# One product per pair of heads for the carried state, shift of 20 weight pieces on ScalarE, in a state-space scan followed by two feed-forward blocks

## The chip, the cores and the metric

The program runs on one core of a Trainium2 chip. The metric is device time in microseconds (us) for one execution; each kernel is executed several times and the median counts. One execution is recorded by the hardware profiler; its rows are the trace. Engines: PE is TensorE's matmul queue and PEld its weight loads, DVE is VectorE, ACT is ScalarE, POOL is GpSimd, SP issues most of the transfers.

## The reference

Three computations follow one another. The first is a state-space scan over 4 batches, 8 heads, 768 positions, head width D = 32 and state width N = 16. In chunks of positions:

```python
M = (Cc @ Bc.T) * L                 # L: causal decays inside the chunk
y = M @ xc + (Cc @ state) * decay_to_i
state = decay_full * state + (Bc * decay_from_j).T @ xc
```

Its output (3072 tokens, 256 features, a head being 32 of them) goes through `g = elu(x @ w_in)`, `x2 = g @ w_out` (256 to 2048 to 256), and then through `((x2 @ w1) * (x2 @ w2)) @ w3 @ wo2` (width 1024).

## The kernel before, in words

**Precision.** Large products are made from a high and a low word of each operand (type fp32r): `mm3` issues three matmuls, low weights by high data, high by low, high by high (lines 382, 383, 384). The small products of the scan are plain fp32 matmuls, and the trace shows each of them as two records.

**Stages.** Six tiles of 512 tokens (NTILE) are each four chunks of 128 positions (CPT); a chunk has two halves `s` of R = 64 positions. For a pair of chunks `unit_u` makes C·B (line 521) and the state increments u (line 556), and `unit_y` makes y: 32 matmuls within the halves (line 590), then 32 that add what the carried state gives (line 598). `made_x` evacuates y from PSUM as high words (ScalarE in the first two tiles, VectorE after) and low words (VectorE); it is letter z, its second step Y. For each tile and each of 8 column blocks n of `w_in`, `unit_a` (letter a) makes h, `elu` its activation in five steps on ScalarE and VectorE, and `unit_b` (b) multiplies by `w_out`. `half_a` (v) is the early form of a: it makes h of the first 256 tokens of tile 0 alone, so that TensorE need not wait for chunks 2 and 3; a later `unit_a` then makes the other half only. The first four column blocks of tile 0 use plain fp32 words in `unit_b` (line 745).

The second half of the program (letters c e g G E ( ) and d) forms the last block by products of sums of blocks: seven `by_product` products per column m of w1 and w2, and `last_product` (d). Results of c, G, E and ) share PSUM room m % 2, so the c of column m+2 waits until `gate_1` (line 902, letter >) of column m has read that room; VectorE runs it in a queue with the sums (lines 893, 896) and the low words (line 162).

**State.** A tile `st` holds the states of 8 heads: 128 partitions are four head pairs of 2 × 16 rows, and the 2 × 32 columns are both heads' features. The product Bx of a pair also fills the blocks that mix the two heads, and these are not wanted. Before, `cd` (C by the decays, made on GpSimd by `at_cd`) is stored with zeros for the other head, 2 × 64 columns per half, and the line 598 product is issued once per head g, with the 32 columns of `st` that belong to it.

**Weights.** They arrive as 44 pieces of 128 × 512 words of 64 bits packed in halves; `shifted` (letter k, VectorE, line 210) and `scaled` (j, ScalarE, line 214) prepare both halves of each word, `joined` (K, VectorE) merges them, `his` (H, ScalarE) takes high words and `los` (I) low words.

**Order.** The string ORDER is written out, one letter per step; `in_order` keeps each engine's instructions in that order. What stands before an instruction on its engine, and what it waits for, thus follows from the string.

Of the kernel before, what the change touches and what calls it, by code (L numbers as in the profile page):

```python
# [37 lines left out]
094AAlU7AlC5Al5UCJCD566l8jCNk5K8JkHND6IjDQjND6KkHNkKQzzYNYzIvzjYNYjkaKjk!HaKXjkxIkNjKarkKMjsHMxKbIrNKxsXrLaHkBjLN8j8vsxX  # L38
BHKuWkPIrbDHMKjkIMKbWINsRXaWHLCNjLBbxCDrCttBjNsCakhVkiyxIrKbXkzsWzMHYYuhKNIaHiXIDbxDNrttjsyVaKzXzkHYYhNVaIxijMrkKbMsHxPL
raINhLjsaxijNhRbxXrLCCiaMSBSBrsBCbshxirLahKBiaxksHrIkbjsxCNKrKuHksbhItDVahtDjijykxirbMKHsMzbzhYPiNYuhKbXHtDtDjkyLaBzIzYY  # L40
INiaxKrXLHbHIsxNkhIRa1jBrMiaCxNCsrKwXxshkNribfsjCXjKHuFhMIatjDHNLIakxCDSiSr1bKxtLNrwsjskykfHFKhIaMzzHKjINibBkMBxYKYbhNri
PsuhbXjDtiXwtkDLykfhFRaHXHIziBNbxIYjLrwzBsNYKukHMfIbjFDMKtHNaDILXCkwxBLCNhtrKajsfjKhiaxiHrkIbFKHxINsrbhskyhSwPjzzYYMKiaH
XSIijMfBakxCFNHCrIaXxsrRwxsrsbfjKkFLahBiuLxbrtBDCHDItbshiKyhHbzXIzYi1CuhYMaDDXttwixMrLBafNLsbBxCFrCkNjsyhazijYkbKxzKr3Y%
&su&h=bitbhtD&D=y=S&Saz=YNziaxYrsaNh3xibxkrrbsshiahjijKbxkK%&ra&s^=hb=&ix&=ar=Nsax1rh3aNxirksb3jxKs@jakK%&=a@#&h3rib&s@&
=x=b=h#Nri^ahs^xia@N#rk#jxsbrKsaSkjSKh%b@i&=xb^h&@=#ahi&ribx#s3r1xsb&=h3^@iar=hbix/srsbh/i|ch_bmi/|#b_/G|e]_gncS[Em({|G}
)]_e>gn<c[*Em(.{G})],<e.>En,g.{*c[,(m)S}*g.1>e.,*G[<3nc,.d*](,mE.}G.{d.,<e],)ng>E,.c{[*dm,(G*.}d.<e]*,d$.d,$),ng>.d+*.(,
[dc,$E}.d@{em,<@d#nG#d*3]g@+)[#^(>E}*c@{e.<dn^dm+d@#G.,)]#*g$>E@(.#^[c{3.d}*m),.e.,G<ng>](,@^E[}c,dm,e.#g.,Gd,*]d{E+n*).
<d.{d[*,(>d)+*c}d+m<e.,2gn>3G[+(]c.}dm,E.3,d.,G.,d,*g{e<dn*)+.(]+2*d.}E.>[d{.c,<2em,).Gn*>g],d.,d.,c[E,md,*({G}*.d<]).e*
>$d,.g*n,c[d.+($,2dm,E.}G.,d]{e$,<)@+gn#d[*(>@E}.*c{e<dn#d.,^)m+d@.g#^@G>.d,@*d+@d#](^.,E[c{*dm}).#G<.>e@#dng]#c[,Em,({G
}g],).,e,*En>d[d+*.d{c<*dm,).+(.*G>.g}.d],<[e+En+2c.,dm{(d}d,G,e]<)$,g.+*dn>2[d,c*.+(.d}*.d,2mE,G*.e{d,n<).,d.>g](,[c,E}  # L50
m*d{e*dnG.)],(.>*d$}E.<g.,d.{[c,<$d+me$,2).g,d+[d>nG.d.d.+c],(mE}d,e{G,nd+]),g<(>.d$[d.Ed{}),<d>,d..,d,dd+++++
"""
HALF = 4
VECTOR_LO = 16
PIECES = [(("w_in", "w_out")[k == "o"], "iioiooiiiiooiooo"[:n].count(k)) for n, k in enumerate("iioiooiiiiooiooo")] + [("wo2", m) for m in range(4)] + [("w3", m) for m in range(16)] + [
# [36 lines left out]
XCOLS = (("x", DM), ("bn", NH * N), ("bt", 2 * R), ("cz", 2 * 2 * R), ("cp", SUB * 2 * R))  # L92
# [3 lines left out]
def kernel(  # L96
# [42 lines left out]
    side = const.tile([P, 2], F32, name="side")  # L139
    sel = act.tile([P, 2, 2, TT], F32R, tag="g", name="sel")[:SUB * CPT, 0, 0].rearrange("p (k s i) -> p k s i", k=CPT, s=SUB)  # L140
    begun = const.tile([P, CPT * SUB, R], F32, tag="begun", name="begun")

    def constants():
# [11 lines left out]
        G.memset(begun, 0.0)  # L155

# [35 lines left out]
    class Piece:  # L192


        def __init__(self, name, src, room, dst):
            self.name, self.src, self.room, self.dst = name, src, room, dst
            self.lo, self.word, self.parts, self.half = G, None, None, 0

# [232 lines left out]
    def at_load(k):  # L431
        c = ck[k]
        all_ = att.tile([P, XC], F32, tag="xbc", name=f"xbc{k}", bufs=4)
# [9 lines left out]
        c["cp"] = cols_["cp"].rearrange("p (s f) -> p s f", s=SUB)  # L443
# [99 lines left out]

    def turned(k, p):

        return (p + k % 2) % 4

    def u_products(k, u):
# [3 lines left out]
        for p in range(4):  # L552
            for s in halves(k):
                rows = slice(R * s, R * s + R)
                to = turned(k, p)
                T.matmul(u[32 * to:32 * to + 32, s], c["bd"][rows, 2 * p:2 * p + 2].rearrange("p h n -> p (h n)"),
                         c["x"][rows, 64 * p:64 * p + 64], start=True, stop=True, skip_group_check=True)

    def states(k, u):
# [4 lines left out]
        for s in halves(k):  # L564
            V.scalar_tensor_tensor(out=new[:, s], in0=state[k, s], scalar=pr_of(k)[:, s, R - 1:R], in1=u[:, s],
                                   op0=ALU.mult, op1=ALU.add)
            state[(k, 1) if s == 0 else (k + CPT, 0)] = new[:, s]

    def first_states(k, u):
# [3 lines left out]
        state[k, 1], state[k + CPT, 0] = new[:, 0], new[:, 1]  # L573
        later("8", next_state, k)

    def next_state(k):

        kept = att.tile([P, 2 * D], F32, tag="kept", name=f"kept{k}", bufs=1)
        G.tensor_tensor(out=kept, in0=state[k, 1], in1=ck[k]["pr"][:, 1, R - 1:R].to_broadcast([P, 2 * D]), op=ALU.mult)
        G.tensor_tensor(out=state[k + CPT, 0], in0=state[k + CPT, 0], in1=kept, op=ALU.add)  # L580

    def y_products(*chunks):
        for k, both in chunks:
            c = ck[k]
            for g in range(2):
                for s in range(SUB):
                    rows = slice(R * s, R * s + R)
                    for q in range(4):
                        h = 2 * q + g
                        T.matmul(both[32 * q:32 * q + 32, s, g], c["x"][rows, D * h:D * h + D], c["L"][rows, h],  # L590
                                 start=g == 0, stop=(k, s) not in state, skip_group_check=True)
# [15 lines left out]
    def by_head(y):  # L607
        return y.rearrange("p s (g i) -> p s g i", g=2)
# [500 lines left out]
```

## Time and profile before

| | us |
|---|---|
| median of 3 runs | 525.79 (524.62 to 525.8) |
| profiled execution | 524.71 |
| span of its trace | 523.0 |
| TensorE busy | 508.8 |
| VectorE busy | 428.8 |
| ScalarE busy | 323.6 |
| GpSimd busy | 204.4 |

The span is what the trace covers; 1.7 us of the profiled execution lie around it. The granted clock of TensorE is 1.0 over the whole span.

### The profile page before, as it was taken

To read this page: it belongs to the slowest core of one execution; us is meant where nothing else is said; L and a number is where in the kernel's file an instruction comes from. 1 tells how busy PE (TensorE), PEld (TensorE's weight loads), DVE (VectorE), ACT (ScalarE), POOL (GpSimd) and SP (SyncE) were. 2 spreads that over 40 slices of the span, in tenths; PEclk is the share of its full clock that TensorE was granted. 3 is DMA by queue.
4 is the path that set the end of the run, shared out by engine and by line. 5 is a ranking of instruction groups with operands and counts; after the bars stand their busy time and mean duration, and the time that the engine had idled before them with its cause. 6 is when DMAs were issued, how large, how long until landed. Compare 5 with 4: busy or idle time off the path is not lost.

```text
span 523.0 us, 10654 instructions
## 1 busy us (share of the span) xinstructions
PE 508.8 (97%) x4330; PEld 411.2 (79%) x4330; DVE 428.8 (82%) x589; ACT 323.6 (62%) x482; POOL 204.4 (39%) x184
## 2 busy tenths in 40 slices
PE   5799999999999999999999999999989999999996
PEld 3675788778888888878788888888777888888885
DVE  6888989879897996867766797869999989988845
ACT  2585587655754385535476787747766577765650
POOL 3223004205430544122203333967477465755401
PEclk9999999999999999999999999999999999999999
DMA  8993473147555635053202321001000110001002
GB/s 297 348 277 132 134 207 126 41 143 235 170 158 150 222 108 174 1 160 104 69 35 77 106 80 47 35 0 61 0 22 21 61 41 20 1 20 41 21 1 80
DMA packets 28177, 52.66 MB, mean 101 GB/s; under 512 B 2304, under 2 KB 10880, under 8 KB 28128
## 3 DMA queue, kind: packets, MB, share of 16 engines
q1 hardware_dynamic: 27984, 51.85, 30.4%
q8 instruction: 34, 0.56, 0.4%
q14 instruction: 15, 0.12, 0.1%
q10 hardware_dynamic: 144, 0.13, 0.1%
HBM read 45.58 MB, written 6.39 MB: 99 GB/s over the span
## 4 chain that ended last, share of the span: by engine, by line
PE 91%; DVE 6%; issue 1%; DMA 0%; ACT 0%; DVEq 0%
PE acc L382 9%; PE acc L384 9%; PE h L382 9%; PE acc L383 9%; PE h L383 9%; PE h L384 9%; PE p L382 4%; PE p L384 3%; PE p L383 3%; PE acc L745 3%; PE p_d L382 2%; PE p_d L384 2%; PE p_d L383 2%; PE p_E L382 2%; PE p_E L383 2%; PE p_E L384 2%
## 5 line engine op out<-in xcount | busy, mean ns | idle before, releaser
L715 ACT ACTIVATE e<-h 128x1024 f32<-128x1024 f32 x48 | 49.2, 1025 | 58.0 <-PE h L384 55.5
L382 PE MATMUL h<-xTh,w_in 128*128 128x512 f32 (+1 forms) x200 | 80.0, 400 | 0.8 <-ACT xTh L685 0.8
L383 PE MATMUL h<-xTl,w_in 128*128 128x512 f32 (+1 forms) x200 | 77.7, 389 | 0.0
L384 PE MATMUL h<-xTh,w_in 128*128 128x512 f32 (+1 forms) x200 | 77.5, 388 | 0.0
L162 DVE TENSOR_TENSOR g<-e,g 128x1024 fp32r<-128x1024 f32 x44 | 60.1, 1370 | 15.5 <-ACT g L727 15.4
L382 PE MATMUL acc<-g,w_out 128*128 128x512 f32 x176 | 69.6, 396 | 0.0
L722 DVE SCALAR_TENSOR_TENSOR e<-e,h 128x1024 f32<-128x1024 f32 x44 | 53.3, 1214 | 19.7 <-ACT e L717 19.6
L384 PE MATMUL acc<-g,w_out 128*128 128x512 f32 x176 | 68.6, 390 | 0.0
L383 PE MATMUL acc<-g,w_out 128*128 128x512 f32 x176 | 68.5, 389 | 0.0
L727 ACT CAST g<-e 128x1024 fp32r<-128x1024 f32 x44 | 46.2, 1049 | 30.0 <-PE acc L384 26.5
L717 ACT ACTIVATE e<-e 128x1024 f32<-128x1024 f32 x48 | 50.7, 1059 | 0.8
L382 PEld LDWEIGHTS h<-xTh,w_in 128*128 128x128 f32 x200 | 38.6, 193 | 9.4 <-issue 1.8
L383 PEld LDWEIGHTS h<-xTl,w_in 128*128 128x128 f32 x200 | 38.5, 193 | 7.8 <-issue 0.7
L384 PEld LDWEIGHTS h<-xTh,w_in 128*128 128x128 f32 x200 | 38.6, 193 | 7.6
L162 POOL TENSOR_TENSOR w<-raw_wc,w 128x512 fp32r<-128x512 f32 x16 | 23.9, 1502 | 51.5 <-ACT w L236 48.6
L536 POOL TENSOR_TENSOR xbc<-xbc,pr 128x256 f32<-128x256 f32 (+1 forms) x24 | 22.9, 965 | 50.9 <-DMA L<-a_cut 30.7
L382 PEld LDWEIGHTS acc<-g,w_out 128*128 128x128 f32 x176 | 33.0, 188 | 7.4
L384 PEld LDWEIGHTS acc<-g,w_out 128*128 128x128 f32 x176 | 33.0, 188 | 7.0
L383 PEld LDWEIGHTS acc<-g,w_out 128*128 128x128 f32 x176 | 33.1, 188 | 6.6
L504 POOL TENSOR_TENSOR xbc<-xbc,L 128x128 f32<-128x128 f32 x24 | 15.1, 634 | 58.1 <-DVE L L498 37.7
L899 POOL TENSOR_TENSOR room_l<-room_l,room_o 128x512 f32<-128x512 f32 x12 | 19.8, 1647 | 32.8 <-DVE room_o L896 19.1
L498 DVE TENSOR_TENSOR_SCAN L<-L,eye 128x512 f32<-128x512 f32 x20 | 27.3, 1368 | 2.0 <-DMA L<-a_cut 2.0
(427 smaller groups left out, 1278.2 us busy)
## 6 DMA issues: line engine op xcount, KB each, us to landing
xbc<-in_xc SPq DMA_DIRECT2D x24, 512.0 KB, 6.3
raw_wc<-in_w3t SPq DMA_DIRECT2D x16, 512.0 KB, 4.3
L<-a_cut SPq DMA_DIRECT2D x40, 128.0 KB, 4.8
raw_wi<-in_w_in SPq DMA_DIRECT2D x8, 512.0 KB, 8.6
raw_wo<-in_w_out SPq DMA_DIRECT2D x8, 512.0 KB, 6.4
x_dram<-x SPq DMA_DIRECT2D x6, 512.0 KB, 4.9
room_s<-x_dram SPq DMA_DIRECT2D x12, 256.0 KB, 4.3
out_t<-out SPq DMA_DIRECT2D x11, 256.0 KB, 2.0
```

The source lines that it names most:

```text
L162: eng.tensor_tensor(out=lo, in0=raw, in1=hi.bitcast(F32), op=ALU.subtract)
L382: T.matmul(out, wlo, xhi, start=first, stop=False, **kw)
L383: T.matmul(out, whi, xlo, start=False, stop=False, **kw)
L384: T.matmul(out, whi, xhi, start=False, stop=last, **kw)
L498: V.tensor_tensor_scan(out=flat, data0=wide, data1=eye.rearrange("p h s -> p (h s)"), initial=0.0, op0=ALU.mult, op1=ALU.add)
L536: G.tensor_tensor(out=c["cd"][:, n:], in0=c["cd"][:, n:], in1=c["pr"].rearrange("p s (o i) -> p s o i", o=1)[:, n:].to_broadcast([P, SUB - ...
L715: A.activation(e, h, AF.Exp)
L717: A.activation(e, e, AF.Relu, scale=-1.0, bias=1.0)
L722: V.scalar_tensor_tensor(out=gt[t, n] if plain else e, in0=e, scalar=-1.0, in1=h, op0=ALU.mult, op1=ALU.max)
L727: A.copy(hi, e)
L745: T.matmul(acc, word_of(n)[:, j, es], g[:, j], start=m == 0, stop=False)
L899: GATE[m % 2].tensor_tensor(out=s["two"], in0=s["two"], in1=s["u2"], op=ALU.mult)
```

## The change

1. The carried-state product (line 598) takes both heads of a pair at once: 64 columns of `st` against one `cd` of 64 columns, without the zeros. So `st` must itself be zero outside each head's block: `own_heads` multiplies it on GpSimd by a mask `own` after each update (letter ?, 24 times). `cd` shrinks from 2 × 64 to 64 columns per half, and each chunk's load from 1024 to 896 columns. The rotation of row groups by `turned` goes away.
2. y is now laid out by feature half f over two chunks rather than by chunk over both halves; `made_x` keeps its size. Rows of `w_in` return to their natural order.
3. For 20 of the 44 weight pieces the shift of the low words runs on ScalarE (`scalar_low`) instead of VectorE.
4. ORDER is another string throughout. The order of weight pieces changes, and so does the place of the steps around the first products.

```diff
-094AAlU7AlC5Al5UCJCD566l8jCNk5K8JkHND6IjDQjND6KkHNkKQzzYNYzIvzjYNYjkaKjk!HaKXjkxIkNjKarkKMjsHMxKbIrNKxsXrLaHkBjLN8j8vsxX
...
+094AAlA75UlAl5UCJl566?jD?k5NDCkJCD6K6?!jN?DHQCK8zIkNHzYjY8NIj8QkvzNzYjYKajNkHKjvkMxKaIrMkKjaKkNsHjLMxbIrMLxNKjakrsXHKIbx
...
+SCALAR_LOW = "11000001001111000110000010001001111100011101"
...
-XCOLS = (("x", DM), ("bn", NH * N), ("bt", 2 * R), ("cz", 2 * 2 * R), ("cp", SUB * 2 * R))
+XCOLS = (("x", DM), ("bn", NH * N), ("bt", 2 * R), ("cz", 2 * 2 * R), ("cp", SUB * R))
...
+        V.tensor_reduce(out=own, in_=head.rearrange("p (b g) -> p g b", g=2), op=ALU.add, axis=AX.X)
...
         def shifted(self):
-            V.tensor_scalar(self.low, self.low, 29, None, op0=ALU.logical_shift_right)
+            if self.scalar_low:
+                A.activation(self.low, self.low, AF.Copy, scale=15 / 16 * 2.0 ** -29 * (1 - 2.0 ** -8))
+            else:
+                V.tensor_scalar(self.low, self.low, 29, None, op0=ALU.logical_shift_right)
             self.one_of_two()
...
+    def own_heads(new):
+        n = new.shape[1]
+        G.tensor_tensor(out=new.rearrange("p s (g d) -> p s g d", g=2), in0=new.rearrange("p s (g d) -> p s g d", g=2),
+                        in1=own.rearrange("p (o g e) -> p o g e", o=1, e=1).to_broadcast([P, n, 2, D]), op=ALU.mult)
...
-        for g in range(2):
-            for s in range(SUB):
-                for k, both in chunks:
-                    for q in range(4) if (k, s) in state else ():
-                        at = turned(k, q)
-                        rows = slice(32 * at, 32 * at + 32)
-                        T.matmul(both[32 * q:32 * q + 32, s, g], state[k, s][rows, D * g:D * g + D], ck[k]["cd"][rows, s, g],
-                                 start=False, stop=True, skip_group_check=True)
+        for s in range(SUB):
+            for n, k in enumerate(chunks):
+                for q in range(4) if (k, s) in state else ():
+                    rows = slice(32 * q, 32 * q + 32)
+                    T.matmul(rooms[q // 2][64 * (q % 2):64 * (q % 2) + 64, s, n], state[k, s][rows], ck[k]["cd"][rows, s],
+                             start=False, stop=True, skip_group_check=True)
```

Three places show what the new string moves. The first is ScalarE near the start: `st` are the first states, `raw_wi` a piece of w_in, `xTh0` the high words of tile 0's y. Before:

```order
L572 COPY st1_211<-f2_138 128x128
L214 ACTIVATE raw_wi0_121<-raw_wi0_121 128x512
L236 CAST w_in0_78<-raw_wi0_121 128x512
L572 COPY st2_248<-acc_f_96 128x128
L214 ACTIVATE raw_wi1_123<-raw_wi1_123 128x512
L214 ACTIVATE raw_wo0_125<-raw_wo0_125 128x512
L572 COPY st3_305<-acc_f_96 128x128
L236 CAST w_in1_79<-raw_wi1_123 128x512
L685 CAST xTh0_364<-f2_138 128x2x2x64
L685 CAST xTh0_364<-acc_f_96 128x2x2x64
```

The same place after the change:

```order
L584 COPY st1_215<-f2_144 128x128
L227 ACTIVATE raw_wi0_127<-raw_wi0_127 128x512
L221 ACTIVATE raw_wi0_127<-raw_wi0_127 128x512
L221 ACTIVATE raw_wi1_129<-raw_wi1_129 128x512
L584 COPY st2_246<-acc_f_98 128x128
L584 COPY st3_249<-acc_f_98 128x128
L227 ACTIVATE raw_wi1_129<-raw_wi1_129 128x512
L249 CAST w_in0_80<-raw_wi0_127 128x512
L696 CAST xTh0_304<-f2_144 128x2x2x64
L249 CAST w_in1_81<-raw_wi1_129 128x512
L696 CAST xTh0_304<-acc_f_98 128x2x2x64
```

Two shifts (line 221) stand on ScalarE, and the letters z of chunks 0 and 1 now stand in ORDER ahead of the second Q (the y of chunks 2 and 3), where before both Q came first.

The second place is TensorE's products h of column block 1 of tile 0. Before, h0_1 is made once by `unit_a` at 512 columns (h0_1_412, 12 matmuls, which `elu` reads), and later the second v makes a second tile of that name; this is where that one begins:

```order
L382 MATMUL h0_3_490<-xTh0_364,w_in3_81 128x512
L383 MATMUL h0_3_490<-xTl0_365,w_in3_81 128x512
L384 MATMUL h0_3_490<-xTh0_364,w_in3_81 128x512
L382 MATMUL h0_1_517<-xTh0_364,w_in1_79 128x256
L383 MATMUL h0_1_517<-xTl0_365,w_in1_79 128x256
L384 MATMUL h0_1_517<-xTh0_364,w_in1_79 128x256
```

After the change the second v stands ahead of that a, and h0_1 follows h0_0 directly, in two halves of 256 columns that are both read:

```order
L395 MATMUL h0_0_367<-xTh0_304,w_in0_80 128x256
L396 MATMUL h0_0_367<-xTl0_305,w_in0_80 128x256
L397 MATMUL h0_0_367<-xTh0_304,w_in0_80 128x256
L395 MATMUL h0_1_409<-xTh0_304,w_in1_81 128x256
L396 MATMUL h0_1_409<-xTl0_305,w_in1_81 128x256
L397 MATMUL h0_1_409<-xTh0_304,w_in1_81 128x256
```

So 12 matmuls of 256 columns (h0_1_517), which no instruction reads, leave the program.

The third place is VectorE in the second half of the program, between `gate_1` of columns 3 and 4 (line 902 before, 914 after). Before:

```order
L902 TENSOR_TENSOR room_l2_3806<-room_l2_3806,p_1_3820 128x512
L162 TENSOR_TENSOR room_h2_4032<-room_i7_3886,room_h2_4032 128x512
L893 TENSOR_TENSOR room_l0_3843<-room_i7_3886,p_0_3819 128x512
L162 TENSOR_TENSOR room_t0_4053<-room_l2_3806,room_t0_4053 128x512
L896 TENSOR_TENSOR room_o7_3880<-room_o7_3880,p_E_3822 128x512
L899 TENSOR_TENSOR room_l0_3843<-room_l0_3843,room_o7_3880 128x512
L162 TENSOR_TENSOR room_t1_4073<-room_i7_3886,room_t1_4073 128x512
L162 TENSOR_TENSOR rooms_g_4079<-room_l2_3806,rooms_g_4079 128x512
L162 TENSOR_TENSOR room_t2_4096<-room_h0_3783,room_t2_4096 128x512
L902 TENSOR_TENSOR room_l0_3843<-room_l0_3843,p_0_3819 128x512
```

After:

```order
L171 TENSOR_TENSOR room_t0_3911<-room_l2_3660,room_t0_3911 128x512
L905 TENSOR_TENSOR room_l0_3697<-room_i7_3744,p_0_3673 128x512
L171 TENSOR_TENSOR room_t1_3922<-room_i7_3744,room_t1_3922 128x512
L908 TENSOR_TENSOR room_o7_3729<-room_o7_3729,p_E_3676 128x512
L911 TENSOR_TENSOR room_l0_3697<-room_l0_3697,room_o7_3729 128x512
L171 TENSOR_TENSOR rooms_g_3928<-room_l2_3660,rooms_g_3928 128x512
L171 TENSOR_TENSOR room_t2_3949<-room_h0_3637,room_t2_3949 128x512
L946 TENSOR_TENSOR out_00_3935<-out_00_3935,acc0_480 128x512
L908 TENSOR_TENSOR room_o7_3729<-room_o7_3729,p_E_3676 128x512
L905 TENSOR_TENSOR room_l1_3749<-room_i7_3744,p_1_3674 128x512
L171 TENSOR_TENSOR rooms_g_3928<-room_l2_3660,rooms_g_3928 128x512
L914 TENSOR_TENSOR room_l0_3697<-room_l0_3697,p_0_3673 128x512
```

Between the two gates stand 8 VectorE instructions before and 11 after (the gate of column 3, room_l2, is the row just ahead of the second list). In the same stretch, from the c of column 5 to the c of column 6, TensorE has 13 products before and 15 after; from there to the c of column 7 it has 11 in both, and VectorE's instructions up to and with the gate of column 5 go from 11 to 8.

## Rows read from the trace of the kernel before

**Rows 1.** Page, busy us of each engine (share of the span), xinstructions.

```profile
PE 508.8 (97%) x4330; PEld 411.2 (79%) x4330; DVE 428.8 (82%) x589; ACT 323.6 (62%) x482; POOL 204.4 (39%) x184
```

**Rows 2.** Waits of TensorE (total, times, longest); its busy us in a window.

```profile
PE p L382 <- DVE room_l L902: 1.8, 2, 1.4
...
0.00:20.71 20.71, 12.49 (x328) 1.00 0.92 330
```

**Rows 3.** Timeline, TensorE at a y and a u block: start us, us, instruction.

```profile
56.95 0.85 PE L598 MATMUL y<-xbc,st 32*32 32x64 f32 x64
57.73 0.50 PE L382 MATMUL acc<-g,w_out 128*128 128x512 f32 x1
...
60.70 0.69 PE L521 MATMUL s<-xbc 32*64 32x128 f32 x32
61.32 0.45 PE L556 MATMUL s<-xbc 64*32 64x64 f32 x32
```

**Rows 4.** Timeline, TensorE at the start.

```profile
19.20 0.33 PE L598 MATMUL f<-xbc,st 32*32 32x64 f32 x4
...
19.31 0.33 PE L598 MATMUL f<-xbc,st 32*32 32x64 f32 x4
...
20.71 0.55 PE L382 MATMUL h<-xTh,w_in 128*128 128x256 f32 x1 [0.83 <-ACT xTh L685]
...
21.73 0.41 PE L382 MATMUL h<-xTh,w_in 128*128 128x256 f32 x1
21.94 0.41 PE L383 MATMUL h<-xTl,w_in 128*128 128x256 f32 x1
```

**Rows 5.** Timeline, TensorE from 34 to 44 us.

```profile
34.40 0.79 PE L382 MATMUL h<-xTh,w_in 128*128 128x512 f32 x1
35.03 0.40 PE L383 MATMUL h<-xTl,w_in 128*128 128x512 f32 x1
35.26 0.39 PE L384 MATMUL h<-xTh,w_in 128*128 128x512 f32 x1
...
37.53 0.28 PE L382 MATMUL h<-xTh,w_in 128*128 128x256 f32 x1
...
39.05 0.80 PE L521 MATMUL s<-xbc 32*64 32x128 f32 x32
...
40.16 3.70 PE L745 MATMUL acc<-g,words_l 128*128 128x512 f32 x8
43.70 3.60 PE L745 MATMUL acc<-g,words_h 128*128 128x512 f32 x8
```

**Rows 6.** Timeline, ScalarE at the start.

```profile
12.46 0.68 ACT L214 ACTIVATE raw_wi<-raw_wi 128x512 f32<-128x512 f32 x1
...
19.92 0.37 ACT L685 CAST xTh<-f 128x256 fp32r<-128x256 f32 x1 [0.82 <-PE acc_f L598]
```

**Rows 7.** Timeline, VectorE at the start.

```profile
12.12 1.21 DVE L498 TENSOR_TENSOR_SCAN L<-acc_f,eye 128x512 f32<-128x512 f32 x1
...
15.04 1.87 DVE L528 TENSOR_TENSOR L<-f,L 128x512 f32<-128x512 f32 x3
```

**Rows 8.** Timeline, GpSimd at the start.

```profile
9.33 0.45 POOL L536 TENSOR_TENSOR xbc<-xbc,pr 128x128 f32<-128x128 f32 x1 [7.54 <-DVE pr L464]
...
15.48 1.31 POOL L162 TENSOR_TENSOR w_in<-raw_wi,w_in 128x512 fp32r<-128x512 f32 x1 [0.18 <-ACT w_in L236]
```

**Rows 9.** Timeline, VectorE at the gates of columns 3, 4 and 5.

```profile
366.48 0.67 DVE L902 TENSOR_TENSOR room_l<-room_l,p 128x512 f32<-128x512 f32 x1
...
374.29 0.67 DVE L902 TENSOR_TENSOR room_l<-room_l,p 128x512 f32<-128x512 f32 x1
...
384.52 0.67 DVE L902 TENSOR_TENSOR room_l<-room_l,p 128x512 f32<-128x512 f32 x1
```

**Rows 10.** Groups by line and shape: busy us, mean ns | idle before, releasers.

```profile
L504 POOL TENSOR_TENSOR xbc<-xbc,L 128x128 f32<-128x128 f32 x24 | 15.1, 634 | 58.1 <-DVE L L498 37.7 <-DMA raw_wo<-in_w_out 17.5 <-issue 2.9
L565 DVE SCALAR_TENSOR_TENSOR st<-st,pr,s 128x64 f32<-128x64 f32 x36 | 9.6, 276 | 2.6 <-PE s L556 2.0
```

More of the change, by code (lines that the diff above doesn't have):

```diff
@@ L139 @@
     side = const.tile([P, 2], F32, name="side")
+    head, own = const.tile([P, NH], F32, name="head"), const.tile([P, 2], F32, name="own")
     sel = act.tile([P, 2, 2, TT], F32R, tag="g", name="sel")[:SUB * CPT, 0, 0].rearrange("p (k s i) -> p k s i", k=CPT, s=SUB)
@@ L567, in states @@
             state[(k, 1) if s == 0 else (k + CPT, 0)] = new[:, s]
+        later("?", own_heads, new[:, :len(halves(k))])
+    def own_heads(new):
+        n = new.shape[1]
+        G.tensor_tensor(out=new.rearrange("p s (g d) -> p s g d", g=2), in0=new.rearrange("p s (g d) -> p s g d", g=2),
+                        in1=own.rearrange("p (o g e) -> p o g e", o=1, e=1).to_broadcast([P, n, 2, D]), op=ALU.mult)
     def first_states(k, u):
@@ L573, in first_states @@
         state[k, 1], state[k + CPT, 0] = new[:, 0], new[:, 1]
+        later("?", own_heads, new)
         later("8", next_state, k)
@@ L578, in next_state, with y_products @@
         kept = att.tile([P, 2 * D], F32, tag="kept", name=f"kept{k}", bufs=1)
-        G.tensor_tensor(out=kept, in0=state[k, 1], in1=ck[k]["pr"][:, 1, R - 1:R].to_broadcast([P, 2 * D]), op=ALU.mult)
+        G.tensor_tensor(out=kept, in0=state[k, 1], in1=pr_of(k)[:, 1, R - 1:R].to_broadcast([P, 2 * D]), op=ALU.mult)
         G.tensor_tensor(out=state[k + CPT, 0], in0=state[k + CPT, 0], in1=kept, op=ALU.add)
-    def y_products(*chunks):
-        for k, both in chunks:
+    def y_products(chunks, rooms):
+        for n, k in enumerate(chunks):
             c = ck[k]
-            for g in range(2):
+            for f, room in enumerate(rooms):
                 for s in range(SUB):
@@ L632, in first_u @@
         for k in ks:
-            u_products(k, ck[k]["room"][0])
+            u_products(k, ck[k]["room"])
         for k in ks:
-            later("6", first_states, k, ck[k]["room"][0])
+            later("6", first_states, k, ck[k]["room"])
     def first_y(*ks):
-        y_products(*((k, ck[k]["room"][1]) for k in ks))
+        at = 2 * R * (1 + ks[0] // 2)
+        rooms = [by_chunk(room[:, :, at:at + 2 * R]) for room in first_rooms[2:]]
+        y_products(ks, rooms)
+        for f in range(2):
+            later("z", made_x, ks[0], f, rooms[f], A)
         for k in ks:
-            later("z", made_x, k, ck[k]["room"][1], A)
             later("M", at_l, CPT + k)
@@ L670, in unit_y @@
     def unit_y(k):
-        two = [(j, by_head(banks(f"y{j}")[:, :, :2 * R])) for j in (k, k + 1)]
-        y_products(*two)
-        for j, both in two:
-            later("z", made_x, j, both, A if j < 2 * CPT else V)
+        rooms = [by_chunk(banks(f"y{k}_{f}")[:, :, :2 * R]) for f in range(2)]
+        y_products((k, k + 1), rooms)
+        for f in range(2):
+            later("z", made_x, k, f, rooms[f], A if k < SCALAR_Z * CPT else V)
         if k % CPT == 0 and k // CPT + 1 < NTILE:
@@ L681, in unit_y, with made_x @@
                 later("X", at_load, j)
-    def made_x(k, both, hi_eng):
-        hi, lo = x_room(k)
+    def made_x(k, f, both, hi_eng):
+        hi, lo = x_room(k, f)
         (A.copy if hi_eng is A else V.tensor_copy)(hi, both)
@@ L1010 @@
         p.lo = V if 0 < n < VECTOR_LO else G
+        p.scalar_low = SCALAR_LOW[n] == "1"
     for k in range(CPT):
@@ L1062 @@
         cz[:, :, :, :, j, :, :, j] = c4[:, :, :, :, j]
-    c2 = C.reshape(NB, 4, 2, CPB, SUB, R, N).transpose(3, 0, 1, 2, 6, 4, 5).copy()
-    c2[:, 1::2] = np.roll(c2[:, 1::2], 1, axis=2)
-    cp = np.zeros(c2.shape[:6] + (2, R), C.dtype)
-    for j in range(2):
-        cp[:, :, :, j, :, :, j] = c2[:, :, :, j]
+    cp = C.reshape(NB, NH, CPB, SUB, R, N).transpose(2, 0, 1, 5, 3, 4)
     def by_chunk(v):
```

91 lines of the change are left out of this document (44 added, 47 removed).

## The prediction

> **What bounds the kernel now.** I read the page first. TensorE is busy 508.8 of 523.0 us, the next engine 428.8 [rows 1]. The chain of waits, the same view read from the end backwards, is almost all TensorE, so I then looked for the 14 us in which TensorE is not busy. The waits of TensorE and its timeline put 8.2 us of it ahead of the first h product at 20.71 (busy 12.49 of 20.71, [rows 2]), which waited for ScalarE's xTh [rows 4], 1.8 us at two places in the second half where VectorE's gate came late [rows 2], and most of the rest behind the last product. Between 21 and 366 us TensorE never waits. So a change can gain in three ways: fewer TensorE instructions, an earlier first h product, a shorter wait at those gates. What it moves between VectorE, ScalarE and GpSimd is worth something only there, and costs something only where it makes TensorE wait anew.
>
> **The carried-state products.** A pair of chunks runs 32 of them, 64 records, in 0.78 us (56.95 to 57.73), 12.2 ns a record [rows 3]. After the change there are 16, 32 records, with 64 columns of weights rather than 32. What does one take? The trace has no such shape with 64 columns of data. Below, 12.2 ns, the pace of the old ones. Above, 19.4 ns, which is line 521 with the same 32*64 weights but twice the data columns (0.62 us for 32 records, [rows 3]). Beyond that I need how many run at once. A record of 512 columns in plain fp32 takes 0.44 us ((43.70 - 40.16)/8, [rows 5]), so one of 64 columns takes 55 ns alone. At 12.2 ns about four and a half run side by side. The old products alternate over two chunks with row groups rotated by `turned`, and so meet 8 distinct places of 32 rows by 32 columns. The new ones meet only four (row group q, column half q % 2). If four do run side by side the price is 55/4 = 13.7 ns. If it is the number of places that sets the parallelism, half as many places give 24.4 ns and nothing is gained. At the start, where 256 columns take 0.21 us and the clock is thus 1.2 GHz (the granted clock reads 1.0 there), the same old products come 8 per 0.11 us, 13.7 ns [rows 4]. There a record alone lasts 110 ns, so eight ran at once, without any spare time per place. At 2.4 GHz the 12.2 ns is therefore the pace at which they are issued, not a limit of the places, and four places should be kept nearly full. I take 13.7 ns: 32 x 13.7 = 0.44 us, a saving of 0.34 us a pair. Ten pairs make **-3.4 us** (between -3.9 at 12.2 ns and 0 at 24.4; -1.6 at 19.4). The two pairs of the first tile have only the second half of each chunk and stand in the start, costed below.
>
> Here a rule speaks against the change. In the old code four row groups write the same PSUM bank at once, and the rate above shows that they overlap. The new code puts row groups 0 and 1 of one half into one bank, 2 and 3 into another. The Trainium skill, "TensorEngine Tiling (Array Packing)", Gotcha 1: PSUM Pressure, says that different row tiles cannot access the same PSUM bank simultaneously; by it only two of the four would run at a time, the 24.4 ns end. By that rule the old products too should have been confined to two at a time (two chunks, one bank each), and the trace does not agree with it.
>
> **Products that no one reads.** The second v of the old order comes after the a that it should have shortened, so 12 matmuls of 256 columns are made for nothing, from 37.53 to 39.05 [rows 5], less a tenth that the passage to the small products takes anyway. They are gone: **-1.4 us**, with no doubt but the place.
>
> **The start.** Before, ScalarE's z for chunk 0 starts at 19.92, released by the last y product of chunks 2 and 3 [rows 6], because both Q stand ahead of it. After, z follows the first Q. The sum for its new date: VectorE's fourth scan began at 12.12 with one decay (0.62) ahead of it [rows 7], which now comes later; with 0.15 for the small reduce of the mask it starts at 11.65 and ends at 12.9. GpSimd then needs 0.45 for B by decay of chunk 3 [rows 8], so that u of chunk 3 is made by 14.1. ScalarE copies the states after its three L214-like steps (12.5 + 3 x 0.6, [rows 6]), by 14.9. GpSimd's two `own_heads` at 0.45 end at 15.6, one cd (0.3), kept and add (0.9) come next, and the low words of w_in0 take 1.31 [rows 8]: 18.1. TensorE does both Q by 17.1 in the meantime (decays at 0.62 each from 12.9), and ScalarE's z of the first pair ends at 17.3. So the first h waits for w_in0's low words and starts at about 18.4 rather than 20.71: **-2.3 us**. Bounds: -3.3 if GpSimd's small ones pass faster, 0 if something on the new GpSimd chain is late. The loads should be no bound there: four chunks' loads lose 64 KB each, and the old kernel found the first piece landed by 12.46 [rows 6]. Five shifts move onto ScalarE in this stretch at 0.6 each; it has until 23 us before the first exponential is due.
>
> **The gates.** In the second half VectorE is full for some 40 us and TensorE is held twice, 0.45 and 1.4 us [rows 2]. Between the gates at 366.48 and 384.52 [rows 9] VectorE does 20 instructions in 18.0 us, 0.90 each, while TensorE has 24 products at 0.69 (three matmuls of 0.23, [rows 5]; 16.6 us). After, it is again 20 instructions against 26 products (17.9 us). But the first 12 of them stand against 15 products: 10.8 against 10.35 us, so about 0.45 us of wait stays, where 1.4 was. Up to the first gate one instruction and one product are added, 0.9 against 0.7, so 0.65 for 0.45. Together 1.1 for 1.8: **-0.7 us**, between -1.8 (all gone) and +1.5 (other gates of the new string come late).
>
> **What costs.** The four plain blocks of tile 0 now each stand alone between h products, where two stood together: one more passage from plain to fp32r, 0.63 against 0.23 us [rows 5]: **+0.4 us**. `own_heads` costs GpSimd 24 x 0.63 (as line 504, [rows 10]), of which the halved cd gives back about 8 us; both hide under TensorE. The 20 shifts hide before and after, as VectorE holds TensorE nowhere ahead of 366 us; on ScalarE, 62% busy, they cost 20 x 0.6 to 0.68 us [rows 6] under the same cover. I price the three at nothing.
>
> The cover of `own_heads` is thinnest at chunks 4 and 5, where only one h block (2.8 us) stands between u and y, and y's own first 32 products (0.8) ahead of those that need the state: 3.6 us. The chain is two decays (1.2), four state updates at 0.28 [rows 10], two masks at 0.63: 3.6 us. It fits if VectorE is free when u ends. All other pairs have at least two blocks.
>
> **Sum:** -3.4 - 1.4 - 2.3 - 0.7 + 0.4 = -7.4 us on the profiled execution's 524.71, so 517.3. The median of the runs lies 1.1 above that execution, the lowest run 0.1 below; I add 0.2 and forecast **517.5**.
>
> **The rivals.**
> (a) Half as many places, half as parallel: the new products take 0.78 us a pair again. For it: the 12.2 ns were measured on eight places, and no row shows four. Against: the slow-clock rate above. Time 517.5 + 3.4 = 520.9. The Tiling page's bank rule gives the same. Chance 0.2.
> (b) The early start is given back: TensorE runs ahead and then waits in 20 to 60 us for VectorE or ScalarE, which has the extra shifts, or for chunk loads. For it: a share of 82% busy on VectorE [rows 1] leaves little room to catch up. Against: no wait there now, and 3 us less of TensorE work is the only thing to absorb. Time 517.5 + 2.3 + 0.5 = 520.3. Chance 0.15.
> (c) Slower: masks in line behind slow things. `own_heads` waits in GpSimd's queue behind the next chunk's B by decay, which itself waits for transfers and scans (line 504 waited 37.7 us for scans, [rows 10]); y then stops TensorE. It needs 7.4 + 1.6 = 9.0 us over ten pairs, 0.9 us each, to be measurably slower; for a typical pair the mask must come 3 us later than reckoned. Time 527.5. Chance 0.05.
> (d) The gates of the new string come later at several places: up to +4 us, 521.5. Chance 0.1.
>
> **Chances and range.** The forecast as such has 0.5. No change to a measurement of this kernel is within 0.3%, 1.6 us. Only (c), or (a), (b) and (d) together, come near: faster 0.91, same 0.04, slower 0.05. For 8 in 10 the range runs from 514.0 (products at 12.2 ns, start -3.3, no gate wait, less 0.6) to 521.8, which takes in (a), (b) and (d) singly.
>
> **What would show it.** In the new trace: a pair's state products in 0.40 to 0.50 us (0.62 and 0.78 speak for the higher bounds); no h product of 256 columns outside the first two column blocks; first h at 17.7 to 19; TensorE's waits for VectorE in the second half about 1 us in all; no wait of y on GpSimd. The forecast is wrong if TensorE waits on GpSimd or VectorE at y blocks by more than 3 us in sum, or if the first h is no earlier.

## The result, and the profile after

The changed kernel takes 520.93 us in the median of 4 runs (520.16 to 521.72), the kernel before 525.79 (4 runs, 524.62 to 526.5): a ratio of 0.9904, 95% interval 0.9885 to 0.9923, a gain of 4.9 us where 8.3 were forecast. The profiled execution took 521.72, the longest of the four, with a span of 520.0 against 523.0; the spans of the other three were 518.4, 519.6 and 518.8. So the two traces differ by 3.0 us, less than the medians do, and the place where an execution can be longer than its neighbours is found below.

The page's busy row, to be set against [rows 1]:

```profile
PE 505.7 (97%) x3978; PEld 407.4 (78%) x3978; DVE 421.5 (81%) x570; ACT 334.7 (64%) x502; POOL 212.9 (41%) x211
```

The work moved as planned: VectorE has 7 us less, ScalarE 11 and GpSimd 8.5 more. TensorE, which sets the time, has 352 records fewer but only 3.1 us less. The timeline of TensorE at the same y block as in [rows 3]:

```profile
50.61 0.86 PE L603 MATMUL y<-L,xbc 64*32 64x64 f32 x64
51.40 0.69 PE L609 MATMUL y<-xbc,st 32*64 32x64 f32 x32
52.02 0.70 PE L757 MATMUL acc<-g,words_l 128*128 128x512 f32 x1
```

From start to start, the 32 records of line 609 take 51.40 to 52.02 = 0.62 us, or 19.4 ns each, where 64 took 0.78. All ten pairs show it; summed over the trace they take 6.23 us where they took 7.93. So the block lost 1.7 us, half of the 3.4 forecast.

The start, TensorE's timeline:

```profile
15.63 0.32 PE L609 MATMUL acc_f<-xbc,st 32*64 32x64 f32 x2
17.34 0.43 PE L603 MATMUL f<-L,xbc 64*32 64x64 f32 x6 [1.39 <-DVE xTl L171]
19.01 0.34 PE L603 MATMUL f<-L,xbc 64*32 64x64 f32 x5 [1.24 <-issue]
...
20.46 0.32 PE L609 MATMUL acc_f<-xbc,st 32*64 32x64 f32 x2
20.71 0.58 PE L395 MATMUL h<-xTh,w_in 128*128 128x256 f32 x1
...
23.65 0.41 PE L396 MATMUL h<-xTl,w_in 128*128 128x256 f32 x1
23.86 0.36 PE L397 MATMUL h<-xTh,w_in 128*128 128x256 f32 x1
24.06 0.28 PE L395 MATMUL h<-xTh,w_in 128*128 128x256 f32 x1
24.18 0.28 PE L396 MATMUL h<-xTl,w_in 128*128 128x256 f32 x1
```

The first h starts at 20.71, exactly as before, but no longer because z is late. ScalarE and GpSimd were about as early as reckoned, and their timelines show the two dates on which the forecast rested:

```profile
15.98 0.37 ACT L696 CAST xTh<-f 128x256 fp32r<-128x256 f32 x1
...
17.11 0.39 ACT L696 CAST xTh<-acc_f 128x256 fp32r<-128x256 f32 x1
...
16.64 1.48 POOL L171 TENSOR_TENSOR w_in<-raw_wi,w_in 128x512 fp32r<-128x512 f32 x1
```

The first pair's z ends at 17.11 + 0.39 = 17.5 (17.3 was reckoned), the low words of w_in0 at 16.64 + 1.48 = 18.1, as reckoned. What is late is the y of chunks 2 and 3, which stands ahead of the first h in TensorE's queue. It writes the same PSUM tiles (f2, acc_f) that the first z and Y read, so it waits for VectorE's xTl until 17.34; it runs six records, stops again for 1.24 us with no releaser but "issue", and goes on at 19.01.

The waits of TensorE over the whole span (us in total, times, longest):

```profile
PE f L603 <- DVE xTl L171: 1.4, 1, 1.4
PE p L395 <- DVE room_l L914: 1.4, 2, 0.9
PE acc_f L562 <- POOL st L578: 1.3, 1, 1.3
PE f L603 <- issue: 1.2, 1, 1.2
```

The second row answers to the first of [rows 2]: 1.4 us at the gates rather than 1.8. But the timeline has many more small pauses between products than before. If every distance over 0.27 us between the starts of two neighbouring matmuls of the second half is taken less the usual 0.23, the sum is 3.2 us before (11 pauses) and 4.2 after (20). The list above has no name for the new ones, but the waits of TensorE's weight loads from 330 us on have. Three of their rows have no counterpart in the trace before:

```profile
PEld p L395 <- ACT p_A L888: 1.4, 3, 0.5
PEld p_d L396 <- DVE rooms_g L171: 0.6, 1, 0.6
PEld p_d L395 <- ACT out L943: 0.4, 1, 0.4
```

Line 888 is ScalarE's copy of the result of c out of its PSUM room (letter m). At three places of the new string the next product for that room stands so close behind that TensorE waits for the copy, some 0.45 us each time.

One more row matters at the start. The DMA queues, in the window from 16 to 17 us:

```profile
q1 hardware_dynamic: 197, 0.38, 102.6%
q8 instruction: 1, 0.02, 6.8%
```

One packet of code (16 KB, 1.1 us of one DMA engine) stands among 197 other packets. That it is TensorE's follows from the number of such packets: queue q8 has 34 in the trace of before, where TensorE has 4330 matmuls and as many weight loads, and 31 after, where it has 3978; in both that is about 256 instructions a packet. In steps of 0.1 us it is listed at 16.5; no other such packet comes between 0 and 21 us. 2.5 us later, at 19.01, the stop named "issue" ends. In the trace of before the packet is listed at 15.2, and the stop of 0.60 us in the first carried-state products ends at 17.71: 2.5 us again. The two stops are in different products, but both come when TensorE has started 222 matmuls (x222 in these rows, its busy us up to just before it goes on, first before and then after the change):

```profile
0.00:17.70 17.70, 10.33 (x222) 1.00 0.90 320
...
0.00:19.00 19.00, 10.34 (x222) 1.00 0.91 322
```

So the place of the stop is a count of instructions, as the end of a loaded piece of code would be, and not something that the 223rd product needs.

### The profile page after: what moved, and what is told of

It is laid out like the page before. It is cut to its first block, busy times and chain, and to the rows that moved or that the text cites. A ratio compares the mean times of both kernels' runs of the same rounds, so it can differ in the third digit from the quotient of the medians.

```text
span 520.0 us, 9955 instructions
## 1 busy us (share of the span) xinstructions
PE 505.7 (97%) x3978; PEld 407.4 (78%) x3978; DVE 421.5 (81%) x570; ACT 334.7 (64%) x502; POOL 212.9 (41%) x211
## 4 chain that ended last, share of the span: by engine, by line
PE 92%; DVE 5%; issue 1%; DMA 0%; ACT 0%; POOL 0%; DVEq 0%
PE acc L395 9%; PE acc L396 9%; PE acc L397 9%; PE h L395 9%; PE h L396 9%; PE h L397 8%; PE p L395 4%; PE p L396 4%; PE p L397 4%; PE acc L757 3%; PE p_d L396 2%; PE p_d L395 2%; PE p_d L397 2%; PE p_E L397 2%; PE p_E L395 2%; PE p_E L396 2%
## 5 line engine op out<-in xcount | busy, mean ns | idle before, releaser
L395 PE MATMUL h<-xTh,w_in 128*128 128x512 f32 (+1 forms) x200 | 78.9, 394 | 0.0
L397 PE MATMUL h<-xTh,w_in 128*128 128x512 f32 (+1 forms) x200 | 76.8, 384 | 0.0
L171 DVE TENSOR_TENSOR g<-e,g 128x1024 fp32r<-128x1024 f32 x44 | 58.5, 1332 | 11.6 <-ACT g L738 11.5
L171 POOL TENSOR_TENSOR w<-raw_wc,w 128x512 fp32r<-128x512 f32 x16 | 25.5, 1598 | 45.0 <-ACT w L249 30.7
L578 POOL TENSOR_TENSOR st<-st,own 128x128 f32<-128x128 f32 (+1 forms) x24 | 11.4, 478 | 69.8 <-DVE st L571 69.2
L911 POOL TENSOR_TENSOR room_l<-room_l,room_o 128x512 f32<-128x512 f32 x12 | 19.2, 1597 | 30.6 <-DVE room_o L908 19.3
```

What stands on the lines that cost most here:

```text
L171: eng.tensor_tensor(out=lo, in0=raw, in1=hi.bitcast(F32), op=ALU.subtract)
L395: T.matmul(out, wlo, xhi, start=first, stop=False, **kw)
L397: T.matmul(out, whi, xhi, start=False, stop=last, **kw)
L911: GATE[m % 2].tensor_tensor(out=s["two"], in0=s["two"], in1=s["u2"], op=ALU.mult)
```

## Experiments

Each kernel is the changed one with one edit; ratios are to the kernel before, run on the same chip. Executions of one kernel scatter by about 2 us, so single terms are read from the traces.

**The second Q earlier.** Does the wait for xTl cost the start?

```diff
-!jN?DHQCK8zIkNHzYjY8NIj8Qkvz
+!jN?DHQCKQ8zIkNHzYjY8NIj8kvz
```

> The changed kernel with the letter Q of chunks 2 and 3 moved ahead of the first two z. Theory A (the second Q waited for the first Y, VectorE's reading of the same PSUM tile, and that alone kept the first h at 20.71): the 1.4 and 1.2 us waits of the second Q go, the first h starts at 18.1 to 18.7, when GpSimd has the low words of w_in0, and the time falls by 1.5 to 2.5 us against the changed kernel, to about 518.5 to 519.5. Rival B (the first h has another bound, weights landing or ScalarE's z): first h at 20 or later, time within 0.7 us of the changed kernel. Rival C (early start given back by waits at 20 to 60 us): first h at 18.5 but the time within 0.7 us of the changed kernel.

Median 522.51 (8 runs), ratio 0.9938 (0.9917 to 0.996), span 520.0. The timeline of TensorE:

```profile
17.11 0.34 PE L603 MATMUL f<-L,xbc 64*32 64x64 f32 x5 [0.87 <-issue]
...
19.42 0.55 PE L395 MATMUL h<-xTh,w_in 128*128 128x256 f32 x1 [0.55 <-ACT xTh L696]
...
24.83 0.41 PE L397 MATMUL h<-xTh,w_in 128*128 128x256 f32 x1
25.05 0.32 PE L395 MATMUL h<-xTh,w_in 128*128 128x256 f32 x1
25.20 0.28 PE L396 MATMUL h<-xTl,w_in 128*128 128x256 f32 x1
```

The wait for xTl is gone and h starts 1.29 us earlier, yet the last matmul starts at 515.54 as it did (515.55), and the median is no shorter either. Most of the gain went to the clock: matmuls of 256 columns follow each other at 0.21 us (the 1.2 GHz level) up to 25.05, against 23.86 after the change, and at 0.12 us (2.4 GHz) from then on. That is 25 slow ones against 15, some 0.9 us; the rest went to longer steps among the first six. Ahead of the first h TensorE now pauses 0.55 us for z, which follows the second Q again and starts at 18.91 rather than 15.98. Nor is the earlier h the edit's doing: the code packet is listed at 14.5 here, and the seventh experiment, with the packet at 14.5 and Q where the change put it, starts h at 19.48. So the wait for xTl was real, but taking it away only put another in its place and shortened nothing.

**Four PSUM banks.** In the changed order four neighbouring records write two banks; here they write four.

```diff
-        for s in range(SUB):
+        for z in range(SUB):
             for n, k in enumerate(chunks):
-                for q in range(4) if (k, s) in state else ():
+                for q in range(4):
+                    s = (q + z) % 2
+                    if (k, s) not in state:
+                        continue
```

> The changed kernel with the state products issued so that four neighbours write four different PSUM banks, same count and sizes. Theory A (the 64 columns of weights set the pace, as in line 521 before, whose 32 records also took 0.62 us): a pair's 32 records stay at 0.60 to 0.64 us. Rival B (row groups that share a bank go one after another): they fall to 0.40 to 0.50 us, and the time by 1.2 to 2.2 us. Rival C (four places instead of eight): unchanged at 0.62, so this run alone does not tell A from C.

Median 521.17 (4 runs), ratio 0.9914 (0.989 to 0.9939). The block in TensorE's timeline:

```profile
51.38 0.69 PE L612 MATMUL y<-xbc,st 32*64 32x64 f32 x32
52.01 0.70 PE L760 MATMUL acc<-g,words_l 128*128 128x512 f32 x1
```

0.63 us, nothing gained. The Trainium skill, "TensorEngine Tiling (Array Packing)", Gotcha 1: PSUM Pressure, says that different row tiles cannot access the same PSUM bank simultaneously. This trace shows no cost of that kind: with two banks among four neighbours the block takes 0.62 us, with four 0.63.

**Half the data per record.** Each product runs twice, over 32 columns of data each; the weights stay 64 columns.

```diff
-                    T.matmul(rooms[q // 2][64 * (q % 2):64 * (q % 2) + 64, s, n], state[k, s][rows], ck[k]["cd"][rows, s],
-                             start=False, stop=True, skip_group_check=True)
+                    for i in range(0, R, 32):
+                        T.matmul(rooms[q // 2][64 * (q % 2):64 * (q % 2) + 64, s, n, i:i + 32], state[k, s][rows],
+                                 ck[k]["cd"][rows, s, i:i + 32], start=False, stop=True, skip_group_check=True)
```

> The changed kernel with each state product issued twice, over 32 data columns each (64 records a pair, same weights loaded twice, same sum of data columns). Theory A (weights of 64 columns set the pace, 19.4 ns a record whatever the data): a pair's block goes from 0.62 to 1.2 to 1.3 us, the span is 6 us longer. Rival C (time on each of the four places goes with data columns): the block stays near 0.62 to 0.75 us, the span within 1.5 us.

One run, 529.04, span 527.3. TensorE's timeline:

```profile
53.65 1.19 PE L610 MATMUL y<-xbc,st 32*64 32x32 f32 x64
54.77 1.12 PE L758 MATMUL acc<-g,words_l 128*128 128x512 f32 x2
```

64 records in 1.12 us are 17.5 ns each. If the number of places set the time, a record with half the data would take half, 9.7 ns. It loses only a tenth. The data hardly count; what the two have in common is weights of 32 rows by 64 columns. (A block of 1.2 to 1.3 us was expected and 6 us of span; it is 1.12, and of the 7.3 us of span 5.0 are the ten blocks and 2.5 a later first h, at 23.22, with the packet at 16.5.)

Two rows shown already say more. Line 521 of the kernel before meets all eight places of 32 by 64 over its two chunks, and takes the same 19.4 ns [rows 3]; so it is not the four places either. And line 603 after the change, with 64 rows by 32 columns, just as many weights, takes 0.79 us for 64 records, 12.3 ns: the pace goes with the columns of the weights, not with their number. These columns are also the PSUM rows that a record writes, and no run tells the loading of the columns from the writing of the rows.

**The shift back on VectorE.** `SCALAR_LOW` all zeros.

```diff
-SCALAR_LOW = "11000001001111000110000010001001111100011101"
+SCALAR_LOW = "00000000000000000000000000000000000000000000"
```

> The changed kernel with all 44 shifts on VectorE again, all else kept. Theory A (the move to ScalarE is hidden, as VectorE holds TensorE nowhere between 21 and 340 us): time within 0.8 us of the changed kernel, VectorE busy some 10 us more. Rival B (VectorE's relief is worth something at the start or in later waits): 1 us or more slower than the changed kernel, with new waits of TensorE for VectorE before 100 us.

Median 522.02 (6 runs), ratio 0.9928 (0.991 to 0.9947), span 520.4; VectorE 429.6 us busy, ScalarE 324.0. TensorE's waits name the only place where it shows:

```profile
PE f L603 <- DVE xTl L171: 3.3, 1, 3.3
```

VectorE's xTl is 2 us later (18.86 against 16.88), but the code packet is listed at 16.7 here, so that by the 2.5 us seen elsewhere TensorE could not have gone on before 19.2 anyway; it went on at 19.32. The first h starts at 21.19 and the end moves by 0.4 us. Beyond the start the shift is worth nothing in this trace, as forecast. The median lies 1.1 us above the changed kernel's, where 0.8 was expected at most, though the two intervals overlap. With xTl this late an early packet could not help either; whether the shift is worth more in such executions is not shown.

**The product per head again**, on the new layout.

```diff
-                    T.matmul(rooms[q // 2][64 * (q % 2):64 * (q % 2) + 64, s, n], state[k, s][rows], ck[k]["cd"][rows, s],
-                             start=False, stop=True, skip_group_check=True)
+                    for g in range(2):
+                        at = 64 * (q % 2) + 32 * g
+                        T.matmul(rooms[q // 2][at:at + 32, s, n], state[k, s][rows, D * g:D * g + D], ck[k]["cd"][rows, s],
+                                 start=False, stop=True, skip_group_check=True)
```

> The changed kernel with the state product issued once per head again (32 columns of weights, 64 records a pair), on the new layout; masks, order and all else kept. Theory A (the gain of the one product per pair of heads is 0.78 - 0.62 us a pair, as weights of 64 columns go at 19.4 ns a record and of 32 at 12.2): the block goes back to 0.77 to 0.80 us, the span is 1.5 to 1.9 us longer than the changed kernel's. Rival B (the new layout or the new places are themselves slower): block above 0.85 us. Rival C (the block is not on the path): span within 0.7 us of the changed kernel.

Median 525.42 (12 runs), ratio 0.9991 (0.9973 to 1.0009), span 524.5: more than expected. TensorE's timeline at the start and at the block:

```profile
19.06 0.31 PE L611 MATMUL f<-xbc,st 32*32 32x64 f32 x1 [3.11 <-issue]
...
22.72 0.58 PE L395 MATMUL h<-xTh,w_in 128*128 128x256 f32 x1
...
54.06 0.88 PE L611 MATMUL y<-xbc,st 32*32 32x64 f32 x64
54.87 0.70 PE L759 MATMUL acc<-g,words_l 128*128 128x512 f32 x1
```

This block takes 0.81 us; over ten pairs 7.97 against 6.23 us, +1.7 as expected. The rest is the start. With more records ahead of it, the end of the loaded code, again after 222 matmuls, now falls into the first state products rather than into the second y:

```profile
0.00:19.05 19.05, 10.07 (x222) 1.00 0.90 319
```

TensorE stands there 3.11 us, until 19.06, 2.5 us after the packet listed at 16.5. The y of chunks 0 and 1 is then itself late, h starts 2.0 us later (22.72), and its slow matmuls cost 0.65 more. Sum: 1.7 + 2.0 + 0.65 = 4.4, and the last matmul starts 4.5 us later.

**The 12 dead products back**: the second v after the a again.

```diff
-KajNkHKjvkMxKaIrMkKj
+KajNkHKjkMxKavIrMkKj
```

> The changed kernel with the second v put back behind the a of column block 1, so that 12 matmuls of 256 columns are made again that nothing reads. Theory A (TensorE has no other slack there): last matmul and span 1.2 to 1.6 us later than the changed kernel. Rival B (they fill a wait that is there anyway): within 0.5 us.

Median 521.75 (7 runs), ratio 0.9939 (0.9916 to 0.9963), span 521.8, 1.8 us longer. In the trace h products take 1.5 us more and the first of them starts 0.36 later (code packet at 16.8). The term of 1.4 us holds in the trace, though the span grew by a little more than the 1.6 expected at most; the median is only 0.8 us longer.

**The old second half of ORDER**: its rows from the by_product columns on are those of before.

```diff
-mi/|b_^G|g]_/e[cnEm(S{g}G[<)]e|>En_*c.{(m,).}G><e],d.En,*S({1g})*.<c[,e.*md,nG.g>](,*.c}[E,m.G{.e,<]),ng>d*[c.E,m*d.{(.,
...
+mi/|b_^/G|e]_gncS[Em({|G})]_e>gn<c[*Em(.{G})],<e.>En,g.{*c[,(m)S}*g.1>e.,*G[<nc,.d*](,mE.}G.{d.,<e],)ng>E,.c{[*dm,(G*.}d
...
```

> The changed kernel with the second half of the order string (from the first c on) taken from the kernel before. Theory A (the new second half costs TensorE 4.2 us of gaps against 3.2 before, by the gaps between matmul starts): gaps go back to 2.9 to 3.5 us, span 0.7 to 1.3 us shorter than the changed kernel, time about 520. Rival B (the gaps depend on when the first half hands over, not on the string): gaps near 4.2 or above, span within 0.5 us or longer.

Median 519.7 (6 runs), ratio 0.9899 (0.9873 to 0.9926), span 517.7: the lowest of all, 2.3 us under the trace after the change, though the interval overlaps that of the changed kernel. The waits and, below them, the start in TensorE's timeline:

```profile
PE p L395 <- DVE room_l L914: 1.8, 2, 1.4
```

```profile
17.30 0.47 PE L603 MATMUL f<-L,xbc 64*32 64x64 f32 x16 [1.40 <-DVE xTl L171]
17.95 0.47 PE L603 MATMUL acc_f<-L,xbc 64*32 64x64 f32 x16 [0.18 <-DVE xTl L171]
...
19.48 0.58 PE L395 MATMUL h<-xTh,w_in 128*128 128x256 f32 x1
...
22.63 0.36 PE L397 MATMUL h<-xTh,w_in 128*128 128x256 f32 x1
22.83 0.28 PE L395 MATMUL h<-xTh,w_in 128*128 128x256 f32 x1
```

The named waits at the gates are longer again, 1.8 us, but the pauses of the second half sum to 3.2, and the weight loads no longer wait for lines 888, 943 and 171: 1.0 us came from there. The other 1.2 come from the start, whose program was not touched: the code packet is listed at 14.5 and no stop named "issue" follows the wait for xTl. There is no pause ahead of the first h either, and the clock rises 1.2 us earlier too, so the early start reaches the end of the program here.

**Without the mask.** `own_heads` returns at once; the 24 multiplications are left out, so y also holds the wrong blocks of the states.

```diff
     def own_heads(new):
+        return
```

> The changed kernel without the 24 multiplications of the state by the mask on GpSimd, so that the mixed blocks of the state stay in and the state's part of y is another one. Theory A (masks are hidden but at the start, where the low words of w_in0 stand behind four of them): span within 0.6 us of the changed kernel, first h at 20.0 to 20.8. Rival B (masks hold up y at the ten later pairs): span 1.5 us or more shorter.

Median 520.99 (4 runs), ratio 0.992 (0.9889 to 0.9951), span 519.1; GpSimd 200.2 us busy. TensorE's waits at the start:

```profile
PE f L604 <- DVE xTl L171: 2.4, 1, 2.4
PE acc_f L562 <- DVE L L511: 1.3, 1, 1.3
```

Where TensorE waited 1.3 us for the masked state, it now waits as long for a scan. The code packet is listed at 14.5, h starts at 20.11, and the second half has the same pauses (4.1). So the 0.9 us of span (0.6 were expected at most) are the start's, and they go with the packet: with the same packet the seventh kernel, masks and all, starts h at 19.48. The mask costs nothing that shows.

**The changed kernel once more**, and **both orders together** (the edits of the first and of the seventh experiment):

> The changed kernel once more, not altered. In the eight experiments so far the one 16 KB packet of TensorE's instruction queue that falls into the first 20 us starts at 14.5 us in three traces and at 16.5 to 16.8 us in five, and where TensorE waits for nothing else it goes on 2.5 to 2.6 us after that start (15.2 and 17.71 in the kernel before, 16.5 and 19.01 in the changed one). Theory A: the packet's time differs from one execution to the next of the same kernel, and the start of the changed kernel was unlucky: this trace shows the packet at 14.5, no wait named issue behind the wait for xTl, the first h product at about 19.5 and a span of about 518.8; and the times of the runs lie in two groups, 1 to 2 us apart. Rival B: the program sets the packet's time: it starts at 16.5 again, first h at 20.7, span 520.0 within 0.3. If the packet starts at 16.5 again, A is not refuted by one trace, but then the spread of the times alone speaks for it.

> The second Q ahead of the first Y (as in the first experiment) and the second half of the order from the kernel before together. Theory A (the two are independent, and the start is set by the code packet and by the clock): the gaps of the second half sum to 3.2 us, as with the old second half alone, against 4.2; the wait for xTl at the second z is gone; with the packet at 14.5 the first h product starts at 19.4 and the span is 518.5 to 519 if the low clock lasts to 25 us again, 517.5 if it ends at 23 as it did with the old second half alone; with the packet at 16.5, first h at 20.7 and 519. So no better than the old second half alone (519.7 us), within 1 us. Rival B: both gains add, 1 us from the gates and 1.3 us from the start: span 516.5, some 518.5 us in the median.

The repeat: median 520.71 (6 runs), ratio 0.9914 (0.9891 to 0.9937), span 520.8; packet at 16.8, "issue" until 19.32, h at 21.01. The trace thus shows the late packet again. But its execution took 522.57, and the six times are 519.95, 520.15, 520.64, 520.78, 522.57 and 522.59: two groups 2 us apart, with the late packet in the longer one. The times of the seventh kernel divide likewise (519.38 to 519.98, and 521.2, 521.45), with the packet at 14.5 in a 519.41. This speaks for a packet time that differs between executions. No two traces of one program show both, but the seventh kernel and the changed one have the same program up to 330 us, and their packets are listed at 14.5 and 16.5; so what stands in the string ahead of the packet does not decide it alone. The kernel before falls into two groups as well: of the 18 executions beside the fifth to eighth experiments, eight took 523.84 to 524.76 and ten 525.63 to 527.11.

Both orders: median 520.99 (6 runs), ratio 0.9919 (0.9897 to 0.9941), span 519.1. Pauses 3.2 us, packet at 14.8, h at 19.79 after the 0.55 us for z, high clock from 25.20. The gates' 1 us arrives and the start's does not, so it is no better than the old second half alone.

## Why the prediction was right, and where it was not

The time and its direction were within the range, but the sum did not come out: the traces differ by 3.0 us where 7.4 were reckoned. One term held, one was half, one came to nothing, one had the wrong sign, and a small cost did not appear. The range took in the result because it had been drawn to take in rivals (a), (b) and (d), not because the terms were right.

- **The carried-state products** (-3.4 forecast, -1.7 measured). The mechanism was right: half the records, and less time for it. The size was off: 13.7 ns rested on the old pace at which records are issued and on four places kept full. A record with 64 columns of weights takes 19.4 ns, the bound that [rows 3] gave by line 521, which has weights of the same shape and twice the data. I had read that row as a matter of data. With half the data the pace is still 17.5 ns, with 32 columns of weights 12.7 (0.81 us for 64). So rival (a) and the bank rule both fail: the block did get shorter, and neither less data nor more banks change it much. That loading the weights is the limit is supported by these rows, not measured by itself. Splitting the product per head again, and nothing else, costs the changed kernel 4.5 us in the trace: 1.7 at the ten pairs, and the rest at the start, where half the records also let TensorE get further before the code runs out.
- **Products that no one reads** (-1.4): right, and put back they cost 1.5.
- **The start** (-2.3 forecast, 0 in the trace). The dates of z and of GpSimd's low words were right to 0.2 us. The step "TensorE does both Q by 17.1" failed: the second y reuses PSUM that the first z and Y still read, which delays it to 17.3, and then the code for it was not there until 19.0. Without the second obstacle h starts at 19.48 (the seventh experiment), so this order allows 1.2 us, not 2.3. How much of it a typical execution keeps is open. The medians are 1.9 us further apart than the traces, as the trace before is of a short execution (1.1 us under its median) and the trace after of a long one (0.8 above); an earlier packet in the typical execution would fit this, but no trace shows it.
- **The first matmuls of h** were not in my sum: though h starts at the same time, the clock rises at 24.06 rather than about 25.5, worth 0.6 us. Before, the step from 0.21 to 0.12 us comes here:

```profile
25.36 0.33 PE L384 MATMUL h<-xTh,w_in 128*128 128x256 f32 x1
25.52 0.28 PE L382 MATMUL h<-xTh,w_in 128*128 128x256 f32 x1
25.64 0.28 PE L383 MATMUL h<-xTl,w_in 128*128 128x256 f32 x1
```

- **The gates** (-0.7 forecast, +1.0 measured). The two waits fell from 1.8 to 1.4 us, less than to the 1.1 reckoned, but the new string adds nine short pauses elsewhere, and ScalarE's copies of c are the longest entry among their waits (1.4 us). The forecast looked at VectorE between the known gates alone, and counting its instructions there says nothing of a wait for ScalarE. The old second half alone gives the 1.0 us back; that is rival (d), at a quarter of its price.
- **The passage** (+0.4 forecast, nothing measured): the count was wrong. A passage of 0.63 us from plain to fp32r stands at three places before (34.40, 46.73, 52.93) and at three after (33.79, 39.96, 55.16); the third plain block of the new order is followed by the small products of `unit_u` instead.
- **Masks, shifts, cd** at nothing: right, but for what the shifts are worth at the start (0.4 us in the trace). Rival (c) did not appear at any pair.

By the trace: -1.7 - 1.4 - 0.6 + 1.0 = -2.7 of the 3.0 us between the two last matmuls; the other 0.3 were not traced to a place.

## What to carry to other kernels

Before halving the number of small matmuls by widening their weights, look for a row with the new weight width: its time per record, not the old one's, was the price here, and to within a tenth whatever its data (32 to 128 columns). When a step is moved forward, follow the PSUM tiles and buffers that it reuses, and ask of an early start what the clock and the engine's own code do there. Traces of two kernels that differ in the date of the code packet cannot be compared at the start without regard to it. A string of steps that is tuned for one place should be compared on every stretch: here half of the new one was better and half worse, and the two could be taken apart.

## What the runs showed of the hardware

- **TensorE's code can arrive late.** In nine of the twelve traces TensorE stops once it has started 222 matmuls, in whichever product that is, and it goes on 2.5 to 2.7 us after the tenth of a us in which the packet is listed (from 15.2 to 17.71 before; 16.5 to 19.01 after; in the experiments 14.5 to 17.11, 16.6 to 19.22, 16.5 to 19.12, 16.5 to 19.06, 16.8 to 19.38, 16.8 to 19.32 and 14.8 to 17.47, in their order). In the other three it waited for xTl at least as long. The DMA engines are 92% busy up to 20.71 us [rows 2]; that this load is the reason is not shown. The Trainium skill, "Runtime: NRT & Kernel Launch", Instruction fetch mechanics, describes such blocks of 16 KiB and calls their cost mostly hidden. After the first h no wait named issue stands in the list of waits, which agrees; at the start it cost 0.6 to 3.1 us.
- **The packet's own time** falls at 14.5 to 14.8 or at 16.5 to 16.8 us in the new kernels. The next packet is listed at 18.8 to 19.7 us where the first is early, and at 21.4 to 22.6 where it is late. What decides between the two is not settled; less load on the queues at that time was not tried.
- **An early start can be lost to the clock.** With a pause of 0.55 us just ahead of the first h, the matmuls reach the 2.4 GHz level at 25.20 in both new kernels that have it, though h began 0.9 to 1.3 us earlier than after the change; without the pause it was 22.83 in the seventh. The kernel before, with a pause of 0.83 us, reached it at 25.52. The pause is not the whole of it: the repeat of the changed kernel has none and reached that level only at 25.62. The granted clock reads 1.00 over all of this stretch, so the pace of the matmuls has to be read instead.
